# Lightning attention and a SMELU feed-forward block on one core: k and q of chunks 8 to 23 are cast into one tile and transposed by a crossbar DMA on SyncE's queue, and all v block copies go to Pool's queue

## The chip, the cores and the metric

One Trainium2 chip, one core. The metric is the device time of one execution in microseconds (us). Single executions of one kernel on one chip differ by 1 to 2%, so every kernel here was timed in rounds beside the kernel before on the same chip.

The engines: TensorE (PE in the profile; PEld is its weight load), VectorE (DVE), ScalarE (ACT), GpSimd (POOL) and SyncE (SP, which only issues DMAs here). All of them take their instructions in program order, each from its own list. "SPq" in the profile is SyncE's own list; "L259" is a line of the kernel file, and the numbers shift by some lines from kernel to kernel.

## The reference, cut to what matters

```python
# q, k, v: (4, 8, 768, 64) f32; lam: one decay per head
for b in range(nb):                       # blocks of 64 positions
    qb, kb, vb = ...
    intra = (qb @ kb^T * Dmask) @ vb      # Dmask: lam ** (i - j), causal
    inter = (qb * lam_pow) @ kv_state
    out = intra + inter
    kv_state = lam ** 64 * kv_state + (kb * rev_pow)^T @ vb
x = out as (3072, 512)
h = x @ w_in                              # 512 -> 2048
g = where(h >= 1, h, where(h <= -1, 0, (h + 1)**2 / 4))
return g @ w_out                          # 2048 -> 512
```

## The kernel before

The kernel cuts the attention into 24 chunks of 128 positions (6 for each of 4 batches). A chunk c goes through these steps: loads of k, q and v (256 KB each), casts of k and q to bf16 on ACT, eight PE transposes of 128x128 into PSUM (`t`), copies of the transposed k into a block layout (`kb`) and a product of the transposed q with a decay table (`qT`) on DVE, score matmuls (`s`), masks (`m`), output matmuls (`o`). From chunk 4 on the scaled v is also copied into a block layout by four small DMAs (`vb`, 32 KB each). Between these stand the two large products of the feed-forward block, `l1` (to `ph`) and `l2` (to `py`), which fill PE for most of the time.

```python
def cast(c, x, e):
    d, nm = ((qs, "qs"), (ks, "ks"))[x]
    t = qkp.tile([128, H, D], BF16, name=nm, tag=nm)
    ...                                   # ACT copy (chunk 0: DVE)
def f_vb(c, g, hi):
    o, i = vi[c % NV][HD[hi], :, g, hi, :], vn[c % NV][HD[g], :, hi, :]
    (nc.gpsimd if c < VP else nc.sync).dma_start(out=o, in_=i)          # VP = 12
def f_t(c):
    ptt[c] = pp_t.tile([128, 2, HP, 128], BF16, name="pt", tag="pt")    # PSUM
    for i, x in ((1, ks), (0, qs)):
        for hp in range(HP):
            nc.tensor.transpose(out=ptt[c][:, i, hp, :], in_=pair(x[c], hp), identity=ident)
def f_kb(c, hi):
    ...
    nc.vector.tensor_copy(kbd[c % NKB][HD[hi], :, :, hi, :], ptt[c][HD[hi], 1]...)
def f_qT(c):
    nc.vector.tensor_tensor(qT[c], ptt[c][:, 0], tab_q[:, c % NCB], op=AX.mult)
```

What stands in which engine's list, and where, is decided by a plan that runs when the kernel is built. Each operation is added with its engine, a duration in ns, a further `extra` until its result is there, the operations that it needs, and a due time; the plan then plays the engines forward, takes on each the ready operation that is due first, and writes the lists in that order. On the chip the lists are fixed: an instruction that is not ready holds up all that stand behind it (e9 below shows it on SyncE's list).

```python
add(key, "SP" if sp else "POOL", 600 if sp else 900 ..., fn, need, due=0, extra=1250 ...)   # issue of a load
add(("vb", c, i), "SP", 600, lambda ...: f_vb(...), need, due=-0.5, extra=2200)             # c >= VP
add(("t", c), "PE", mm(*[128] * 8), lambda c=c: f_t(c), [casts, kb and qT of c - 1], due=od - 9000, extra=FILL)
```

Of the kernel before, what the change touches and what calls it, by code (L numbers as in the profile page):

```python
# [9 lines left out]
BF16 = mybir.dt.bfloat16  # L10
I32 = mybir.dt.int32
AX = mybir.AluOpType
# [11 lines left out]
def kernel(  # L24
# [16 lines left out]
    nc = tc.nc  # L41
    B, H, S, D = q.shape
    C = 128
    NCB = S // C
    HP = H // 2
# [8 lines left out]
    CPS = MS // C  # L54

    PLAIN, KA = 4, 1
# [4 lines left out]
    const = ctx.enter_context(tc.tile_pool(name="const", bufs=1))  # L61
    big = ctx.enter_context(tc.tile_pool(name="big", bufs=1))
    ld = ctx.enter_context(tc.tile_pool(name="ld", bufs=LD))
    qkp = ctx.enter_context(tc.tile_pool(name="qkp", bufs=3))
    qtp = ctx.enter_context(tc.tile_pool(name="qtp", bufs=3))
    scp = ctx.enter_context(tc.tile_pool(name="scp", bufs=4))
    xp = ctx.enter_context(tc.tile_pool(name="xp", bufs=3))
# [2 lines left out]
    op = ctx.enter_context(tc.tile_pool(name="op", bufs=3))  # L70
# [30 lines left out]
    NKB, NUB, NV = 3, 3, 4  # L101
    kbd = [const.tile([128, HP, 2, 2, D], BF16, name=f"kbd{i}") for i in range(NKB)]
# [28 lines left out]
    for hi in range(2):  # L131
        nc.scalar.activation(out=ln_t[64 * hi:64 * hi + 64], func=AF.Ln,
                             in_=lam_b[64 * hi:64 * hi + 64].rearrange("p (a b) -> p a b", b=2)[:, :, hi])
# [5 lines left out]
    tab_q = const.tile([128, NCB, HP, 128], F32)  # L139
# [20 lines left out]


    spin = pp_y.tile([128, MS], F32, name="py", tag="py")
    LAT, FILL, SLACK, DSLACK, AHEAD = 70, 170, 400, 2500, 5000
    ops, OPS = [], {}

    class Op:
# [3 lines left out]
    def add(key, eng, ns, fn, needs=(), due=None, extra=0):  # L170
        OPS[key] = Op(key, eng, ns, fn, needs, due, extra)
        ops.append(OPS[key])

    def run_plan(free):

        users = {x.key: [] for x in ops}
        for x in ops:
            x.needs = [OPS[y] for y in x.keys if y in OPS]
            for y in x.needs:
                users[y.key].append(x)  # L180
        left = {x.key: len(x.needs) for x in ops}
        topo = [x for x in ops if not x.needs]
        for x in topo:
            for u in users[x.key]:
                left[u.key] -= 1
                if left[u.key] == 0:
                    topo.append(u)
        assert len(topo) == len(ops)
        for x in reversed(topo):
            d = [u.due - u.ns - x.extra - LAT for u in users[x.key] if u.eng not in ("DMA", "SP")]  # L190
            x.due = min(d + ([x.own] if x.own is not None else []), default=1e9)
            if x.eng in ("DMA", "SP") or x.key[0] in ("l1", "l2", "li", "wi", "zv"):
                x.due = x.own
        left = {x.key: len(x.needs) for x in ops}
        ready = {e: [] for e in free}
        for x in topo:
            if not x.needs:
                ready[x.eng].append((0, x))
        out_seq, pool_end = [], 0
        while len(out_seq) < len(ops):  # L200
            t, e = min((max(free[e], min(r for r, _ in lst)), e) for e, lst in ready.items() if lst)
            r, x = min(((r, x) for r, x in ready[e] if r <= t), key=lambda p: (p[1].due, p[0]))
            ready[e].remove((r, x))
            ns = x.ns
            if e == "DVE" and t < pool_end:
                if x.key[0] == "g1":
                    ns += pool_end - t
                elif x.key[0] in ("g2", "g"):
                    ns += min(ns, (pool_end - t) / 2)
            if e == "POOL":  # L210
                pool_end = t + ns
            free[e] = t + ns
            x.t, x.end = t, t + ns + x.extra
            out_seq.append((t, len(out_seq), x))
            for u in users[x.key]:
                left[u.key] -= 1
                if left[u.key] == 0:
                    lat = SLACK if u.eng == "PE" and x.end > 30000 else DSLACK if u.eng == "SP" else LAT
                    rel = u.own - AHEAD if u.key[0] == "t" and u.key[1] >= CPS else 0
                    ready[u.eng].append((max([rel] + [y.t if y.eng == u.eng else y.end + lat for y in u.needs]), u))  # L220
        pe_end = 1500
        for t, _, x in sorted(out_seq, key=lambda p: p[:2]):
            if x.eng == "PE":
                if x.key[0] == "l2":
                    pe_end = 1e9
                for _ in range(int((t - pe_end - 60) // (216 if t > 8000 else 430))):
                    nc.tensor.matmul(spin, lhsT=idle[:, 0:128], rhs=idle, start=True, stop=True)
                pe_end = max(pe_end, t + x.ns)
            if DBG:
                print(f"{t / 1e3:9.3f} {x.due / 1e3:9.3f} {x.eng:5s} {x.ns:6.0f} {x.key}")  # L230
            x.fn()

    def mm(*cols):
        return sum(c / 2.4 + 3 for c in cols)


    qs, ks, qT, sc_sb, xT, ptt, pst, pot = {}, {}, {}, {}, {}, {}, {}, {}
    pu = [None]
    HD = [slice(0, 64), slice(64, 128)]

# [1 line left out]
        return t[:, 2 * hp:2 * hp + 2, :].rearrange("p a d -> p (a d)")  # L242

    def cast(c, x, e):
        d, nm = ((qs, "qs"), (ks, "ks"))[x]
        t = qkp.tile([128, H, D], BF16, name=nm, tag=nm)
        if e == "ACT":
            nc.scalar.copy(out=t, in_=qkv_ld[c, x])  # L248
        else:
            nc.vector.tensor_tensor(t, qkv_ld[c, x], qkv_ld[c, x], op=AX.max)  # L250
        d[c] = t

    def cast_v(c):
        nc.gpsimd.tensor_tensor(vn[c % NV].rearrange("p a b d -> p (a b) d"), qkv_ld[c, 2],  # L254
                                _bc(tab_k[:, c % NCB, :], 2, D), op=AX.mult)

    VP = 12

    def f_vb(c, g, hi):  # L259
        o, i = vi[c % NV][HD[hi], :, g, hi, :], vn[c % NV][HD[g], :, hi, :]  # L260
# [1 line left out]

    def f_t(c):
        ptt[c] = pp_t.tile([128, 2, HP, 128], BF16, name="pt", tag="pt")
        for i, x in ((1, ks), (0, qs)):
            for hp in range(HP):
                nc.tensor.transpose(out=ptt[c][:, i, hp, :], in_=pair(x[c], hp), identity=ident)  # L267

    def f_kb(c, hi):
        if c < PLAIN:  # L270
            (nc.scalar.copy if c < KA else nc.vector.tensor_copy)(out=kplain(c), in_=ptt[c][:, 1])  # L271
        else:
            nc.vector.tensor_copy(kbd[c % NKB][HD[hi], :, :, hi, :], ptt[c][HD[hi], 1].rearrange("p a (b d) -> p a b d", b=2))  # L273

    def kplain(c):
        return kbd[c % NKB][:, 0:2].rearrange("p a b c d -> p (a b c d)").rearrange("p (h k) -> p h k", k=128)

    def f_qT(c):
        qT[c] = qtp.tile([128, HP, 128], BF16, name="qT", tag="qT")
        nc.vector.tensor_tensor(qT[c], ptt[c][:, 0], tab_q[:, c % NCB], op=AX.mult)  # L280

    def f_u(c):
        if c % NCB == 0:
# [103 lines left out]
        nc.sync.dma_start(out=out[m0:m0 + 128, :], in_=osb[s, ms])  # L387


    T0, STEP, LEAD = 24000, 1047, 3000  # L390
    PARTS = (4, 4, 4, 2, 2, 2)
    l1_order, l2_order = [], []
    for s in range(NST):
        if s == 0:
            o = [(0, 0), (1, 0), (0, 4), (1, 4), (2, 0), (2, 4), (0, 8), (1, 8), (2, 8), (2, 12), (0, 12), (1, 12), (3, 0), (3, 4), (3, 8), (3, 12)]
        else:
            o = [(p, i) for p in range(PARTS[s]) for i in range(0, FO, PARTS[s])]
        l1_order += [(s, i, p) for p, i in o]
        o = [(ms, kg) for ms in range(CPS) for kg in range(CPS)]
        if s == 0:  # L400
            o = [(ms, kg) for kg in range(CPS) for ms in range(2)] + o[FO // 2:]
# [9 lines left out]
    def o_due(c):  # L411
        s, i = c // CPS, c % CPS
        w = CPS // PARTS[s]
        return l_due[1, s, 0, i // w] - LEAD - (w - 1 - i % w) * 8 * STEP
# [14 lines left out]
    for kind, i in order:  # L429
        for x in (1, 0, 2) if kind == "c" else (0,):  # L430
            sp = kind == "c" and not (0 < i < SW or (i, x) == (0, 2))
            if kind == "w":
                key, land, ns, fn, need = ("wi", i), ("w", i), 2800, lambda i=i: load_w(i), []
            else:
                key, land, ns, fn = ("li", i, x), ("ld", i, x), 1060 if sp else 720 if i < 2 else 800, lambda i=i, x=x: f_load(i, x)
                need = [("cast", i - LD, x), ("w", 7) if i == SW else None]
# [18 lines left out]
    for c in range(NCH):  # L455
        od, cb = o_due(c), c % NCB
        lastu = c - 1 if cb else c - 2
        for x in (1, 0):
            e = "DVE" if c == 0 else "ACT"
            add(("cast", c, x), e, 690 if e == "DVE" else 615, lambda c=c, x=x, e=e: cast(c, x, e),  # L460
                [("ld", c, x), ("t", c - 3), ("u", c - 3), ("cast", c - 1, x)])
        for hp in range(HP) if c < NCB and c % 2 == 0 else ():
            add(("tab", c, hp), "ACT", 410, lambda c=c, hp=hp: tabq(c, hp), [("tab", c, hp - 1), (None, ("kb", 0, 0), ("x", 1))[c // 2]])
        add(("cast", c, 2), "POOL", 1060, lambda c=c: cast_v(c),
# [1 line left out]
        for i in range(4 if c >= PLAIN else 0):  # L466
            need = [("cast", c, 2), ("o", c - NV), ("zv", c % NV)]
            if c < VP:
                add(("vb", c, i), "POOL", 640, lambda c=c, i=i: f_vb(c, i // 2, i % 2), need, extra=2800)
            else:  # L470
                add(("vb", c, i), "SP", 600, lambda c=c, i=i: f_vb(c, i // 2, i % 2), need, due=-0.5, extra=2200)
        add(("t", c), "PE", mm(*[128] * 8), lambda c=c: f_t(c),
            [("cast", c, 0), ("cast", c, 1), ("kb", c - 1, 0), ("kb", c - 1, 1), ("qT", c - 1)], due=od - 9000, extra=FILL)
        for hi in range(1 if c < PLAIN else 2):
            add(("kb", c, hi), "ACT" if c < KA else "DVE", 590 if c < KA else 430 if c < PLAIN else 415, lambda c=c, hi=hi: f_kb(c, hi), [("t", c), ("s", c - NKB, 1), ("z", "kb", c % NKB) if c >= PLAIN else None])
        add(("qT", c), "DVE", 690, lambda c=c: f_qT(c), [("t", c), ("o", c - 3), ("qT", c - 1)] + [("tab", c // 2 * 2, hp) for hp in range(HP) if c < NCB])
        if cb < NCB - 1:
            add(("u", c), "PE", mm(*[128] * 4), lambda c=c: f_u(c),
                [("cast", c, 1), ("cast", c, 2), ("ub", lastu, 0), ("ub", lastu, 1), ("u", lastu)], due=od - 6000, extra=FILL)
# [66 lines left out]
```

## Time and profile before

| | kernel before |
|---|---|
| time, median of 3 (range) | 229.05 us (228.72 to 229.09) |
| profiled span | 227.0 us |
| PE busy | 217.0 us, 96% |
| eight PE transposes on the chain of waits | 0.45 us |
| v block copies issued by Pool / SyncE | 32 / 48 |

The page of the kernel before: the busy times, and rows of the span in 40 slices of 5.7 us (a digit is the busy share in tenths; PEclk is the granted TensorE clock in tenths; DMA is the mean busy share of the 16 DMA engines).

```profile
span 227.0 us, 5657 instructions
PE 217.0 (96%) x2272; PEld 158.7 (70%) x2308; DVE 159.5 (70%) x276; ACT 136.6 (60%) x249; POOL 74.0 (33%) x95
...
PE   7799999989999999999999999999999999999993
...
PEclk9999999999999999999999999999999999999999
DMA  5999998969999999497687732112101101110212
...
q1 hardware_dynamic: 71632, 21.77, 38.8%
q0 software_dynamic: 6768, 10.23, 20.5%
...
PE 78%; DVE 12%; POOL 4%; DMA 3%; issue 1%; ACT 0%; POOLq 0%; ACTq 0%
```

PE is busy 80% or more in every slice from 11 us on but the last, at full clock, and the chain of waits (its last line here) is PE for 78%. The DMA engines are full, too, for most of the first 16 slices (91 us): loads, weights and copies. PE waited only 0.2 us for them.

The windows view of the kernel before, 20 us each. Columns: stretch, its length, then busy us and number of instructions of PE, PEld, DVE, ACT and POOL, granted clock, DMA share, GB/s.

```profile
60.00:80.00 20.00, 19.47 (x276) 16.13 (x279) 19.08 (x28) 16.05 (x33) 15.37 (x20) 1.00 1.09 256
80.00:100.00 20.00, 19.49 (x266) 15.69 (x268) 18.82 (x35) 14.23 (x26) 4.04 (x3) 1.00 0.87 204
```

Three pieces of the chain in order of time (start, length, what; 54 to 62 us):

```profile
54.95 1.79 PE ph L339 x32
...
57.94 0.89 PE ph L339 x16
58.83 0.45 PE pt L267 x8
```

The group table gives 219 ns to a transposing matmul, which is its pipelined latency; on the chain eight of them take 0.45 us, and that is what PE gets back if they go.

### The profile page before, as it was taken

The numbers are of one execution on the slowest core, as the hardware profiler recorded it, in microseconds if no ns is written. First come the engines' busy times: TensorE is split into PE (matmuls) and PEld (weight loads), VectorE is DVE, ScalarE is ACT, GpSimd is POOL, SyncE is SP. The second block draws the span as 40 slices with busy tenths as digits, with TensorE's granted clock in tenths as the row PEclk, the third lists the DMA queues.
The fourth block names the chain that finished last, engine by engine and source line by source line (L and its number), as shares of the span: only waits on it lengthen the run. The fifth ranks groups of instructions, "written<-read, shape, count | busy, mean of one in ns | idle before, by whom it ended". The sixth has DMA issues, their size and how long they took to land.

```text
span 227.0 us, 5657 instructions
## 1 busy us (share of the span) xinstructions
PE 217.0 (96%) x2272; PEld 158.7 (70%) x2308; DVE 159.5 (70%) x276; ACT 136.6 (60%) x249; POOL 74.0 (33%) x95
## 2 busy tenths in 40 slices
PE   7799999989999999999999999999999999999993
PEld 2467888867787778877877777776777776766441
DVE  6635889998689998996678687783875775544300
ACT  6768575844988667588547648645565554545121
POOL 8999765956899420221032210000000000000000
PEclk9999999999999999999999999999999999999999
DMA  5999998969999999497687732112101101110212
GB/s 147 232 255 212 268 204 220 201 144 275 269 253 272 243 271 238 76 241 155 163 194 149 198 88 70 37 35 69 48 3 46 49 0 49 48 46 3 92 46 92
DMA packets 78570, 32.36 MB, mean 143 GB/s; under 512 B 69648, under 2 KB 73744, under 8 KB 78544
## 3 DMA queue, kind: packets, MB, share of 16 engines
q1 hardware_dynamic: 71632, 21.77, 38.8%
q0 software_dynamic: 6768, 10.23, 20.5%
q8 instruction: 18, 0.29, 0.5%
q14 instruction: 8, 0.07, 0.1%
q10 hardware_dynamic: 144, 0.00, 0.0%
HBM read 27.27 MB, written 6.29 MB: 148 GB/s over the span
## 4 chain that ended last, share of the span: by engine, by line
PE 78%; DVE 12%; POOL 4%; DMA 3%; issue 1%; ACT 0%; POOLq 0%; ACTq 0%
PE ph L339 32%; PE py L378 32%; PE pt L267 4%; DVE gT L372 3%; DMA w_in_sb<-in_moe_w_in_dram 3%; PE ps L298 3%; DVE t L353 3%; PE po L322 2%; DVE w L357 2%; PE po L316 2%; PE pu L286 2%; DVE sc L309 1%; POOL x2f L420 1%; DVE kbd L273 1%; POOL vn L254 1%
## 5 line engine op out<-in xcount | busy, mean ns | idle before, releaser
L347 ACT ACTIVATE r<-ph,one 128x512 bf16<-128x512 f32 x96 | 65.8, 687 | 60.5 <-PE ph L339 42.2
L339 PE MATMUL ph<-xT,w_in_sb 128*128 128x128 bf16 (+1 forms) x1152 | 98.9, 237 | 0.2 <-DMA w_in_sb<-in_moe_w_in_dram 0.2
L339 PEld LDWEIGHTS <-w_in_sb 128*128 128x128 bf16 x1152 | 81.7, 98 | 15.5 <-DMA w_in_sb<-in_moe_w_in_dram 0.4
L378 PE MATMUL py<-w_out_sb,gT 128*128 128x512 bf16 x351 | 89.8, 379 | 1.7
L378 PEld LDWEIGHTS <-gT 128*128 128x128 bf16 x384 | 34.6, 98 | 27.5
L254 POOL TENSOR_TENSOR vn<-x2f,tab_k 128x512 bf16<-128x512 f32 x24 | 27.6, 1151 | 52.2 <-DMA vi<-vn 22.7
L353 DVE TENSOR_SCALAR t<-r 128x1024 bf16<-128x1024 bf16 x48 | 25.3, 526 | 23.8 <-ACT r L347 23.7
L372 DVE TENSOR_TENSOR gT<-w,t 128x1024 bf16<-128x1024 bf16 x48 | 37.3, 778 | 1.1
L357 DVE TENSOR_TENSOR w<-r,t 128x1024 bf16<-128x1024 bf16 x48 | 35.4, 738 | 1.4
L309 DVE TENSOR_TENSOR sc<-ps,causal 128x512 bf16<-128x512 f32 (+1 forms) x40 | 22.1, 553 | 7.4 <-PE ps L298 7.4
L383 ACT COPY osb<-py 128x512 f32<-128x512 f32 x24 | 14.0, 585 | 15.7 <-PE py L378 15.2
L273 DVE COPY kbd<-pt 64x512 bf16<-64x512 bf16 x40 | 16.8, 419 | 7.1 <-PE pt L267 6.7
L261 POOL DMA_DIRECT2D vi<-vn x32 | 20.2, 647 | 2.7 <-POOL vn L254 2.4
L280 DVE TENSOR_TENSOR qT<-pt,tab_q 128x512 bf16<-128x512 bf16 x24 | 16.6, 690 | 1.7 <-ACT kbd L271 1.1
L329 ACT CAST xT<-po 128x512 bf16<-128x512 f32 x24 | 14.0, 583 | 5.6 <-PE po L322 4.1
L290 ACT CAST ubd<-pu 64x256 bf16<-64x256 f32 x40 | 14.6, 365 | 2.4 <-PE pu L286 2.1
L248 ACT CAST qs<-x0f 128x512 bf16<-128x512 f32 x23 | 14.2, 618 | 0.7 <-DMA x0f<-in_q_dram 0.7
L298 PE MATMUL ps<-qT,kbd 128*128 128x128 bf16 (+1 forms) x160 | 13.3, 206 | 1.4 <-DVE qT L280 0.8
L248 ACT CAST ks<-x1f 128x512 bf16<-128x512 f32 x23 | 14.2, 616 | 0.1
L316 PE MATMUL po<-qT,ubd 128*128 128x128 bf16 x80 | 13.8, 221 | 0.0
L298 PEld LDWEIGHTS <-kbd 128*128 128x128 bf16 x160 | 10.5, 98 | 4.4 <-issue 1.5
L322 PE MATMUL po<-sc,vi 128*128 128x128 bf16 (+1 forms) x160 | 13.2, 206 | 0.1
(50 smaller groups left out, 136.2 us busy)
## 6 DMA issues: line engine op xcount, KB each, us to landing
out_dram<-osb SPq DMA_DIRECT2D x24, 256.0 KB, 2.0
x1f<-in_k_dram SPq DMA_DIRECT2D x18, 256.0 KB, 4.1
x0f<-in_q_dram SPq DMA_DIRECT2D x18, 256.0 KB, 4.3
x2f<-in_v_dram SPq DMA_DIRECT2D x17, 256.0 KB, 4.1
w_in_sb<-in_moe_w_in_dram POOLq DMA_DIRECT2D x4, 512.0 KB, 7.5
w_out_sb<-in_moe_w_out_dram POOLq DMA_DIRECT2D x4, 512.0 KB, 9.8
x2f<-in_v_dram POOLq DMA_DIRECT2D x7, 256.0 KB, 4.7
x1f<-in_k_dram POOLq DMA_DIRECT2D x6, 256.0 KB, 6.6
```

What stands on the lines that cost most here:

```text
L248: nc.scalar.copy(out=t, in_=qkv_ld[c, x])
L254: nc.gpsimd.tensor_tensor(vn[c % NV].rearrange("p a b d -> p (a b) d"), qkv_ld[c, 2], _bc(tab_k[:, c % NCB, :], 2, D), op=AX.mult)
L261: (nc.gpsimd if c < VP else nc.sync).dma_start(out=o, in_=i)
L273: nc.vector.tensor_copy(kbd[c % NKB][HD[hi], :, :, hi, :], ptt[c][HD[hi], 1].rearrange("p a (b d) -> p a b d", b=2))
L298: nc.tensor.matmul(pst[c, g][:, hp, :], lhsT=kbd[c % NKB][:, hp, g].rearrange("p a d -> p (a d)"), rhs=qT[c][:, hp, 64 * g:], start=True, ...
L309: nc.vector.tensor_tensor(sc_sb[c][g], pst[c, g], _bc(causal[:, 0:128 - 64 * g], 1, HP), op=AX.mult)
L339: nc.tensor.matmul(ph[:, j * m:(j + 1) * m], lhsT=w_in_sb[:, ko, (i + j) * 128:(i + j + 1) * 128], rhs=xT[s][:, ko, p * m:(p + 1) * m], st ...
L347: nc.scalar.activation(out=r_t[grp][:, i, :], in_=ph_t[s, ni, part], func=AF.Relu, bias=one[:, 0:1])
L353: nc.vector.tensor_scalar(t_t[grp], r_t[grp], 0.5, 1.0, op0=AX.mult, op1=AX.min)
L357: nc.vector.tensor_tensor(w_t[grp], r_t[grp], t_t[grp], op=AX.subtract)
L372: nc.vector.tensor_tensor(o, w, t, op=AX.mult)
L378: nc.tensor.matmul(py_t[s, ms], lhsT=gT[s][:, ko, ms * 128:(ms + 1) * 128], rhs=w_out_sb[:, ko, :], start=(ko == 0), stop=(ko == FO - 1))
```

## The change

Intent: PE is full, DMA has been carrying less from 100 us on, so the transposes of chunks 8 to 23 move from PE to the DMA crossbar. k and q share one tile so that one DMA of 256 KB does both. The result lies in SBUF in place of PSUM, which should make DVE's copies cheaper. The v block copies leave SyncE's queue to make room for the transposes.

```diff
-    qkp = ctx.enter_context(tc.tile_pool(name="qkp", bufs=3))
+    NQK, NXT, XT = 4, 2, 8
+    qkp = ctx.enter_context(tc.tile_pool(name="qkp", bufs=NQK))
+    xtp = ctx.enter_context(tc.tile_pool(name="xtp", bufs=NXT))
...
+    def f_xt(c):
+        t = xtp.tile([128, 2, HP, 128], BF16, name="xq", tag="xq")
+        ptt[c] = t
+        nc.sync.dma_start_transpose(out=t..., in_=qk[c].rearrange("p a h d -> p (a h d)"))
...
-    VP = 12
+    VP = 24
...
-    T0, STEP, LEAD = 24000, 1047, 3000
+    T0, STEP, LEAD = 24000, 1015, 3000
...
+        if c < XT:
+            add(t, "PE", mm(*[128] * 8), lambda c=c: f_t(c), need, due=od - 9000, extra=FILL)
+        else:
+            add(t, "SP", 1250, lambda c=c: f_xt(c), need, due=-0.7, extra=3500)
```

Cut: the shared tile `qk` in the casts and their due times, the release of a transpose 16 us (of plan time) before the chunk's output is due at the earliest, the DVE durations told to the plan.

## The prediction

> **What bounds the kernel now.** TensorE (PE). The page's first part has PE busy 217.0 us of the 227.0 us span at a granted clock of 0.999. The chain of waits is PE for 78%, and after 85 us almost nothing else. VectorE (DVE) is the second limit: 12% of the chain, in two stretches, about 38 to 48 and 68 to 85 us. The windows view has DVE busy 42.8 of 47 us between 38 and 85 us, but 57.3 of 75 between 85 and 160; Pool 33.1, then 9.5.
>
> **What the change takes away.** 128 transposing matmuls and their weight loads (16 chunks of 8); the built program's order shows exactly these 256 PE instructions gone. The group table gives 219 ns for one, but that is pipelined latency: on the chain eight take 0.45 us. So 16 x 0.45 = 7.2 us of PE time. About 14 of the 16 lie after 80 us, where PE bounds: 6.3 us. The plan's pace constant falls by 32 ns over 192 steps, 6.1 us, which agrees.
>
> DVE's k copies (32 half-tiles at 419 ns from PSUM) now read SBUF. A one-source SBUF copy of twice the row length takes 408 to 426 ns here, so I estimate 0.26 us: 5 us less DVE work. The q product stays at 690 ns.
>
> **What it adds.** 16 crossbar transposes of 256 KB on SyncE's queue. The Trainium skill (VectorE: DVE Perf Modes, "The three transpose paths") gives 1309 ns for a 128x128 block by DMA; no transpose is in this trace, so the cost of eight blocks is open. The nearest things are stores landing in 2.0 us and loads in 4.1 to 4.3. I estimate 3 to 6 us from issue to landing, hidden: the plan releases it 14 us before the chunk's output is due, about 8 us before its scores.
>
> 48 block copies of v move to Pool at 0.64 us each: 31 us more Pool work, mostly between 75 and 165 us, where Pool has room. DVE pays: the skill (SBUF — State Buffer, "Who interferes with whom") says that Pool and DVE's fast modes lock each other out of a shared port. The trace agrees: DVE's three gate steps take 0.43, 0.69 and 0.69 us while Pool is quiet, up to 2.05, 1.41 and 2.26 while it works. Their excess is about 11 us for some 42 us of Pool work after 20 us, so 31 us more should cost about 8 us, less the 5 saved. DVE goes from 76% to perhaps 80 to 85% after 85 us: below PE, with a few longer stalls.
>
> **On the critical path.** 7.2 us off; I give back 0.5 to 1 us for copies drawn into the DVE-bound stretch and for jitter. Predicted: 222.7 us (-2.8%), range 219.8 to 227.0. Faster by over 2% (below 224.5): 0.68; within 2%: 0.25; slower by over 2%: 0.07.
>
> **What would show it.** PE busy about 210 us, the chain after 85 us still PE; transposing matmuls down from 192 to 64; Pool busy about 105 us; k copies from chunk 8 near 0.26 us; more long gate steps after 85 us; transposes landing within 6 us, and score matmuls waiting little for qT. Wrong if score matmuls wait for transposes, PE shows over 2 us more idle, or SyncE's stores and loads stand behind transposes.
>
> **What would make it wrong.** Transposes that take 8 us or more, or hold up the loads on DMA engines that are full (share about 1.0) until 85 us; Pool falling behind, since a chunk's copies and scaling need about 3.7 us of it and DVE can block it; DVE stalls on Pool reaching PE between 68 and 100 us. Better than predicted if cheaper k copies shorten the DVE-bound stretch.

## More of the kernel before

32 matmuls of `l1` take 1.79 us, 16 take 0.89.

And two lines of SyncE's timeline, with 17 loads between them (start, length of the issue, what):

```profile
59.17 1.03 SPq L420 DMA_DIRECT2D x0f<-in_q_dram  x1
...
79.75 0.78 SPq L420 DMA_DIRECT2D x0f<-in_q_dram  x1
```

From 59.17 to 79.75 us SyncE issues nothing but prefetch loads, one every 1.14 us (20.58 us over 18). The plan reckons with 0.6. In this kernel PE waits for none of these loads.

## The result, and the profile after

The changed kernel took 237.54 us (median of 4, 236.64 to 238.51) beside 229.07 us for the kernel before: 1.037 times the time (95% interval 1.033 to 1.042). All four runs count as fast, at a mean granted clock of 0.971 to 0.983. Ratios here and below are the mean time of one kernel's fast runs over that of the other's of the same rounds, so not quite the ratio of the medians that are quoted.

```profile
span 236.7 us, 5411 instructions
PE 217.4 (92%) x2180; PEld 154.8 (65%) x2180; DVE 159.5 (67%) x276; ACT 137.3 (58%) x249; POOL 104.4 (44%) x143
...
PE   7897999999994794898999999999999999999993
...
PEclk9999999999999799799999999999999999999999
DMA  5999997969999999999999514372433011100212
...
q1 hardware_dynamic: 75472, 24.39, 46.4%
...
PE 56%; DMA 18%; DVE 17%; POOL 3%; ACT 2%; issue 1%; SPq 0%; ACTq 0%; POOLq 0%
PE py L386 24%; PE ph L347 23%; DMA xq<-qk 11%; DVE w L365 4%; DVE t L361 4%; DMA w_in_sb<-in_moe_w_in_dram 4%; DVE gT L380 3%; DVE sc L317 2%; PE ps L306 2%; DVE kbd L281 2%; DMA x2f<-in_v_dram 2%; PE po L330 2%; DVE qT L288 2%; PE po L324 1%; DMA vi<-vn 1%
```

The chain is now PE for 56% only, and 11% of it is the new transposes (`DMA xq<-qk`). PE has two holes between 71 and 95 us (the digits 4, 7, 9, 4), the clock dips as each ends, and the DMA engines stay full six slices longer, to 130 us. The same stretches as before:

```profile
60.00:80.00 20.00, 14.68 (x190) 11.56 (x188) 12.60 (x20) 13.97 (x27) 14.30 (x20) 0.97 1.11 248
80.00:100.00 20.00, 15.72 (x170) 12.14 (x169) 9.93 (x19) 8.61 (x16) 7.14 (x10) 0.86 1.22 251
```

PE lost 4.8 us of work between 60 and 80 us and 3.8 us between 80 and 100 us against before, and from 80 to 100 us the mean clock was 0.86. What PE waited for, by the view of waits (line, releaser: us in total, times, longest), and what DVE waited for:

```profile
PE ps L306 <- DVE qT L288: 10.1, 4, 5.3
```

```profile
DVE kbd L281 <- DMA xq<-qk: 17.0, 5, 6.7
```

The kernel before had 0.8 us of the first and of course none of the second. Now the two long waits in PE's timeline (start, length, what, and in brackets the idle time before it and its releaser):

```profile
78.68 0.58 PE L306 MATMUL ps<-qT,kbd 128*128 128x128 bf16 x4 [5.26 <-DVE qT L288]
79.06 1.91 PE L386 MATMUL py<-w_out_sb,gT 128*128 128x512 bf16 x4
80.77 1.69 PE L347 MATMUL ph<-xT,w_in_sb 128*128 128x128 bf16 x16
82.30 0.28 PE L306 MATMUL ps<-qT,kbd 128*128 128x64 bf16 x4
...
95.70 0.60 PE L306 MATMUL ps<-qT,kbd 128*128 128x128 bf16 x4 [4.16 <-DVE qT L288]
96.10 3.41 PE L347 MATMUL ph<-xT,w_in_sb 128*128 128x128 bf16 x32
```

Waits of 5.26 and 4.16 us, both for `qT` of a chunk whose transpose had just landed. And after each of them PE runs at half speed for a while: 16 matmuls of `l1` start at 80.77 and are followed by the next group at 82.30, 1.53 us, where 16 of them took 0.89 us in the kernel before; 32 take 3.25 us from the start at 96.10 to that of the next group, in place of 1.79. Over the stretches 78.7 to 82.3 and 95.7 to 99.4 us that costs some 3 us (the sum of these differences and that of the four `py` matmuls, 1.71 for 0.86). The Trainium skill (TensorE: Matmul & The Clock Gate, "What's actually happening") says that TensorE falls to half clock after an idle window of about 3.4 us and comes back after a busy one of about 3.4 us; this trace agrees, with idle times of 5.3 and 4.2 us and half speed for 3.6 us after each (the windows view has a clock of 0.50 from 97 to 99 us and 1.00 from 99.4 us on). In the other traces of this case the bound is less sharp: all 13 waits of PE over 4 us were followed by half clock, but so was one of 2.59 us (e6), while one of 3.69 us (e9) was not.

So why did the transposes come late? The last cast of chunk 8 on ACT, then SyncE's own timeline:

```profile
61.57 0.62 ACT L252 CAST qk<-x0f 128x512 bf16<-128x512 f32 x1
```

```profile
66.17 2.29 SPq L428 DMA_DIRECT2D x1f<-in_k_dram  x1
...
70.56 1.29 SPq L428 DMA_DIRECT2D x1f<-in_k_dram  x1
71.93 1.99 SPq L259 DMA_TRANSPOSE xq<-qk  x1
...
77.84 1.99 SPq L259 DMA_TRANSPOSE xq<-qk  x1
```

And all transposes (counts, ns, first and last start; the first line is SyncE's own waiting before them):

```profile
L259 SPq EVENT_SEMAPHORE  x16: 17/17/28, 71.9 to 180.9; - x16
L259 SPq DMA_TRANSPOSE xq<-qk x16: 1293/1359/3207, 71.9 to 181.0; - x16
...
DMA to landing us min/median/max: 2.7/4.4/6.7
```

The casts of chunk 8's k and q were done by 62.2 us. Its transpose was issued at 71.93 us, because SyncE was issuing prefetch loads back to back, about 1 us each, and the transpose stood behind them in the list; once it was at the head it did not wait (17 to 28 ns). The plan's own listing puts that transpose at 61.0 us of plan time, behind loads reckoned at 600 ns of issue each. The shortest issue of a load takes 0.37 us in these traces, and a store's takes 0.34 us in the quiet after 140 us; between 50 and 126 us, with the DMA engines full, a load's takes a median of 0.85 us plus about 0.1 us until the next. Over twenty loads SyncE falls some 10 us behind its plan. The landing itself takes 2.7 to 6.7 us, median 4.4. A late transpose holds up ACT as well as DVE: a cast writes one of four shared `qk` tiles and must wait until the transpose that reads it has landed (10.9 us of ACT's waiting here).

What the prediction foresaw did happen beside this: Pool is busy 104.4 us, the k copies from SBUF have a median of 291 ns, and DVE's three gate steps cost 102.5 us in place of 98.0.

### The profile page after: what moved, and what is told of

It is laid out like the page before. It is cut to its first block, busy times and chain, and to the rows that moved or that the text cites. A ratio compares the mean times of both kernels' runs of the same rounds, so it can differ in the third digit from the quotient of the medians.

```text
span 236.7 us, 5411 instructions
## 1 busy us (share of the span) xinstructions
PE 217.4 (92%) x2180; PEld 154.8 (65%) x2180; DVE 159.5 (67%) x276; ACT 137.3 (58%) x249; POOL 104.4 (44%) x143
## 3 DMA queue, kind: packets, MB, share of 16 engines
q1 hardware_dynamic: 75472, 24.39, 46.4%
## 4 chain that ended last, share of the span: by engine, by line
PE 56%; DMA 18%; DVE 17%; POOL 3%; ACT 2%; issue 1%; SPq 0%; ACTq 0%; POOLq 0%
PE py L386 24%; PE ph L347 23%; DMA xq<-qk 11%; DVE w L365 4%; DVE t L361 4%; DMA w_in_sb<-in_moe_w_in_dram 4%; DVE gT L380 3%; DVE sc L317 2%; PE ps L306 2%; DVE kbd L281 2%; DMA x2f<-in_v_dram 2%; PE po L330 2%; DVE qT L288 2%; PE po L324 1%; DMA vi<-vn 1%
## 5 line engine op out<-in xcount | busy, mean ns | idle before, releaser
L347 PE MATMUL ph<-xT,w_in_sb 128*128 128x128 bf16 (+1 forms) x1152 | 101.3, 240 | 2.8 <-DMA w_in_sb<-in_moe_w_in_dram 1.9
L386 PE MATMUL py<-w_out_sb,gT 128*128 128x512 bf16 x384 | 96.3, 382 | 0.0
L347 PEld LDWEIGHTS <-w_in_sb 128*128 128x128 bf16 x1152 | 83.7, 100 | 18.0 <-DMA w_in_sb<-in_moe_w_in_dram 2.2
L269 POOL DMA_DIRECT2D vi<-vn x80 | 50.3, 645 | 54.6 <-issue 49.6
L361 DVE TENSOR_SCALAR t<-r 128x1024 bf16<-128x1024 bf16 x48 | 26.6, 554 | 23.6 <-ACT r L355 23.5
L365 DVE TENSOR_TENSOR w<-r,t 128x1024 bf16<-128x1024 bf16 x48 | 38.5, 802 | 1.3
L306 PE MATMUL ps<-qT,kbd 128*128 128x128 bf16 (+1 forms) x160 | 13.7, 210 | 10.7 <-DVE qT L288 10.1
L281 DVE COPY kbd<-xq 64x512 bf16<-64x512 bf16 x32 | 10.4, 325 | 17.4 <-DMA xq<-qk 17.0
L252 ACT CAST qk<-x1f 128x512 bf16<-128x512 f32 x23 | 14.2, 618 | 11.2 <-DMA xq<-qk 10.9
L252 ACT CAST qk<-x0f 128x512 bf16<-128x512 f32 x23 | 14.1, 619 | 0.2 <-DMA x0f<-in_q_dram 0.2
L229 PE MATMUL py<-idle 128*128 128x512 bf16 x36 | 11.6, 462 | 1.2 <-DVE one L117 1.2
```

The lines of the kernel that those rows point to most:

```text
L252: nc.scalar.copy(out=t, in_=qkv_ld[c, x])
L306: nc.tensor.matmul(pst[c, g][:, hp, :], lhsT=kbd[c % NKB][:, hp, g].rearrange("p a d -> p (a d)"), rhs=qT[c][:, hp, 64 * g:], start=True, ...
L347: nc.tensor.matmul(ph[:, j * m:(j + 1) * m], lhsT=w_in_sb[:, ko, (i + j) * 128:(i + j + 1) * 128], rhs=xT[s][:, ko, p * m:(p + 1) * m], st ...
L361: nc.vector.tensor_scalar(t_t[grp], r_t[grp], 0.5, 1.0, op0=AX.mult, op1=AX.min)
L365: nc.vector.tensor_tensor(w_t[grp], r_t[grp], t_t[grp], op=AX.subtract)
L386: nc.tensor.matmul(py_t[s, ms], lhsT=gT[s][:, ko, ms * 128:(ms + 1) * 128], rhs=w_out_sb[:, ko, :], start=(ko == 0), stop=(ko == FO - 1))
```

## The experiments

Theories, formed after reading the trace:

- **Q**: the transposes stand too late in SyncE's in-order list, behind loads that the full DMA engines accept at 1 us each and not at 0.6.
- **P**: the 31 us of extra Pool issues lock DVE out, and that starves PE.
- **L**: a landing time of 4.4 us hurts wherever the transpose stands.
- **D**: the DMA engines cannot carry loads and transposes together.
- **R** (formed later): what matters is the order of the compute engines, not SyncE's.

Eighteen kernels ran, all with correct results. Overview (median us of all runs, with the slow ones in e3, e4, e6, e9, e11, e15, e16 and e17; ratio of fast runs to the kernel before on the same chip, 95% interval; PE's total wait for `qT` in the profiled run):

| run | edit to the changed kernel | us | ratio | wait for qT |
|---|---|---|---|---|
| (changed) | none | 237.5 | 1.037 (1.033 to 1.042) | 10.1 |
| e1 | transposes back on PE, v copies on Pool | 229.9 | 1.008 (0.999 to 1.018) | none listed |
| e2 | v copies back on SyncE | 242.9 | 1.063 (1.056 to 1.071) | 12.0 |
| e3 | plan: load issue 1050 | 230.4 | 1.007 (0.997 to 1.016) | 5.9 |
| e4 | transposes from chunk 14 on | 235.4 | 1.028 (1.017 to 1.038) | 8.8 |
| e5 | transposes on ScalarE's queue | 249.9 | 1.091 (1.085 to 1.098) | 0.5 |
| e6 | e4 with load issue 1050 | 230.0 | 1.002 (0.993 to 1.011) | 2.7 |
| **e7** | plan: load 1150, transpose 2000 + 5000 | **222.3** | **0.970 (0.962 to 0.977)** | none listed |
| e8 | e7, transposes from chunk 12 on | 224.9 | 0.982 (0.977 to 0.988) | 0.6 |
| e9 | SyncE's order of e7, others as changed | 259.1 | 1.127 (1.116 to 1.138) | 0.7 |
| e10 | SyncE's order as changed, others of e7 | 235.8 | 1.028 (1.020 to 1.036) | 1.0 |
| e11 | plan: load 1150 only | 226.2 | 0.978 (0.968 to 0.989) | 0.3 |
| e12 | plan: transpose 2000 + 5000 only | 234.9 | 1.022 (1.015 to 1.030) | 8.4 |
| e13 | every transpose six places earlier | 240.7 | 1.049 (1.041 to 1.058) | 8.4 |
| e14 | e7 with v copies back on SyncE | 224.6 | 0.977 (0.969 to 0.985) | 1.0 |
| e15 | e5 with slower loads in the plan | 231.2 | 0.999 (0.988 to 1.010) | 1.4 |
| e16 | transposes of chunks 8 to 13 earlier | 239.0 | 1.042 (1.031 to 1.052) | 0.2 (see below) |
| e17 | transposes of chunks 8 to 16 earlier | 230.0 | 1.002 (0.995 to 1.010) | 1.5 |
| e18 | e7 again, five rounds | 222.8 | 0.972 (0.966 to 0.978) | 0.8 |

The profiled runs of e3, e4 and e15 fell in the slow state of those kernels' runs (over 1.5% above their fastest); their traces are read for which wait stands where, and the ratios use fast runs alone.

### e1_pool_only: the v copies alone

```diff
-    NQK, NXT, XT = 4, 2, 8
+    NQK, NXT, XT = 4, 2, 24
```

> All chunks are transposed by TensorE again (128 transposing matmuls back); only the 48 v block copies stay moved to Pool, with the one tile for k and q. Theory Q (the crossbar transposes stand behind prefetched loads in SyncE's in-order queue and reach PE late): no transposes, so 228 to 231 us and PE's wait for qT near zero, as before. Theory P (Pool's 31 us of extra issues lock DVE out, and that starves PE): 234 us or more, with DVE's gate steps long between 80 and 150 us.

229.9 us, ratio 1.008: within the noise of the kernel before, with 31 us more Pool work. P is out. This run also gives what a transpose costs the DMA engines, as it differs from the changed kernel's traffic by the 16 transposes alone:

```profile
span 226.6 us, 5611 instructions
...
q1 hardware_dynamic: 58576, 20.19, 34.5%
q0 software_dynamic: 8304, 11.80, 23.3%
```

SyncE's queue took 34.5% of 226.6 us here, 78.2 us of all sixteen engines, for 77 loads and stores of 256 KB: 1.02 us each. In the changed kernel it took 46.4% of 236.7 us, 109.8 us. The 16 transposes are the difference, 31.6 us: **1.98 us of packet time on all sixteen engines for each transpose of 256 KB**, about twice a load. (Packets that wait for each other are counted in full, as a share of 1.22 shows, so this is rather too much than too little; e5 gives a second value.)

### e2_xt_only: the transposes alone

```diff
-    VP = 24
+    VP = 12
```

> The 16 crossbar transposes stay, the 48 v block copies go back to SyncE's queue, where they take 0.6 us of issue each. Theory Q: the loss stays, 235 to 245 us, with PE waiting about 10 us for qT between 70 and 100 us; it may grow, as the copies share the transposes' queue. Theory P: the loss goes, 222 to 226 us.

242.9 us: the loss stays and grows, PE waits 12.0 us for `qT`. It is the transposes, and freeing SyncE's queue of the v copies helped them, as the change intended.

### e3_li1050: one number of the plan

```diff
-            add(key, "SP" if sp else "POOL", 600 if sp else ...
+            add(key, "SP" if sp else "POOL", (1050 if i else 600) if sp else ...
```

> The changed kernel with one number of its plan altered: an issue of a load on SyncE is reckoned at 1050 ns, about what the trace shows while DMA engines are full, in place of 600. No work is added or taken away; the transpose of chunk 8 has 17 SyncE instructions ahead of it, not 23. Theory Q: the first transpose is issued by 66 us (71.9 in the changed kernel), PE's waits for qT fall from 10.1 to under 3 us, and the time is 221 to 227 us. Theory P, or a theory L that a transpose's 4.4 us of landing is what hurts wherever it stands: within 1% of 237.5 us.

230.4 us, ratio 1.007. The first transpose was issued at 67.7 us and PE's waits fell to 5.9 us: 3% back by reordering alone, which speaks for Q against P and L, though less than Q expected (under 3 us, 221 to 227 us).

### e4_xt14: start later

```diff
-    NQK, NXT, XT = 4, 2, 8
+    NQK, NXT, XT = 4, 2, 14
```

> Crossbar transposes only from chunk 14 on (10 in place of 16), all v copies on Pool as in the changed kernel. Most of these are due after 105 us, when the DMA engines' share falls below 0.8 and few loads remain. Theory Q: PE's wait for qT under 1.5 us; 10 x 0.45 us = 4.5 us of PE time saved against before, so 224 to 226.5 us. Theory P: still 232 us or more. Theory L: each transpose still lands late, 228 us or more.

A miss for the way I had put Q: 235.4 us. The quiet of the DMA engines that I had counted on did not come in time (they were full until about 118 us in this trace), and SyncE's list had fallen behind by then. The first transpose, chunk 14's, was issued at 110.85 us after an unbroken run of loads and a few stores, and PE's one long wait was 7.32 us just before that chunk's scores; after it there was none over 1.2 us. Q has to be said more exactly: the lag of SyncE's list grows with every load, and whatever stands behind the loads gets all of it.

### e5_act_queue: another queue

```diff
-        nc.sync.dma_start_transpose(...)
+        nc.scalar.dma_start_transpose(...)
-            add(t, "SP", 1250, lambda c=c: f_xt(c), need, due=-0.7, extra=3500)
+            add(t, "ACT", 1250, lambda c=c: f_xt(c), need, extra=3500)
```

> The 16 crossbar transposes are issued by ScalarE on its own queue, in its order of work, in place of SyncE's queue; everything else is the changed kernel's. Theory Q (place in SyncE's in-order queue): a transpose no longer waits its turn behind loads, so chunk 8's is issued by about 65 us, PE waits for qT under 2 us in all, 221 to 227 us, though ScalarE gives some 1.3 us of issue for each. Theory D (the DMA engines are full, and each transpose takes about 2 us of all sixteen of them wherever it is issued): transposes still land 4 to 6 us late and PE still waits over 5 us for qT, 232 us or more.

Both theories missed. Chunk 8's transpose was issued at 64.2 us and the wait for `qT` went (0.5 us), as Q said; but the time was 249.9 us. Now ACT stood with casts at the head of its list, 20.7 us for transposes that had to free a `qk` tile and 7.8 us for the loads x0f and x1f, and what PE waited for stood behind them.

```profile
PE pu L294 <- ACT ubd L298: 12.3, 4, 6.7
```

The transposes landed after 5.0 us (median), no faster than on SyncE's queue. Alone on ACT's queue, their packets took 10.2% of 248.5 us, 1.58 us for each (1.83 us in e15), which is less than the difference in e1 gives. The Trainium skill (DMA: Bandwidth & Descriptors, "Issuing engines are not separate DMA queues") says that DMAs of all issuing engines run on the same 16 engines and interleave, so that several issuers only save issue time; this run agrees.

### e6_li1050_xt14 and e8_li1150_xt2000_from12: later starts with a corrected plan

e6 is e4 plus e3's edit; e8 is e7 (next) with `XT = 12`.

> e4_xt14 (transposes from chunk 14 on) with the plan's issue of a load on SyncE reckoned at 1050 ns in place of 600, as in e3. Theory Q: the one long wait of e4 (7.3 us before chunk 14's scores) falls under 2 us and the time to 224 to 228 us. Theory D: a wait of 5 us or more stays, 232 us or more.

> As e7, with transposes from chunk 12 on (12 of them). Theory Q and D both: less DMA work before 100 us, PE's wait for qT under 2 us, and 12 x 0.45 = 5.4 us of PE time off the kernel before: 223.5 to 226.5 us. If PE still waits over 4 us for qT, neither an accurate order nor a later start cures it.

e6: 230.0 us, the 7.3 us wait fell to 2.6 us; better than e4 by 2.5%, though short of 224 to 228. e8: 224.9 us, as expected; that it is slower than e7 fits twelve transposes saving less PE time than sixteen.

### e7_li1150_xt2000: the plan told what the DMA engines do

```diff
-            add(key, "SP" if sp else "POOL", 600 if sp else ...
+            add(key, "SP" if sp else "POOL", (1150 if i else 600) if sp else ...
-            add(t, "SP", 1250, lambda c=c: f_xt(c), need, due=-0.7, extra=3500)
+            add(t, "SP", 2000, lambda c=c: f_xt(c), need, due=-0.7, extra=5000)
```

> The changed kernel (16 transposes from chunk 8 on) with its plan told what the full DMA engines do: 1150 ns for an issue of a load on SyncE, 2000 ns for that of a transpose and 5000 ns more until it has landed (600, 1250 and 3500 in the changed kernel). Only the order of instructions changes. Theory Q: PE's wait for qT falls from e3's 5.9 us to under 3, 223 to 228 us. Theory D: no better than e3's 230 us, as loads then come late in place of transposes.

222.3 us, ratio 0.970: faster than both kernels, with the same instructions and the same bytes as the changed kernel, in another order.

```profile
span 218.2 us, 5364 instructions
PE 209.5 (96%) x2148; PEld 151.5 (69%) x2180; DVE 157.6 (72%) x276; ACT 137.1 (63%) x249; POOL 104.8 (48%) x143
...
PEclk9999999999999999999999999999999999999999
DMA  5999999668999999999999999925532110111112
```

```profile
63.03 3.47 SPq L259 DMA_TRANSPOSE xq<-qk  x1
...
67.22 2.11 SPq L259 DMA_TRANSPOSE xq<-qk  x1
```

The transpose of chunk 8 now goes out at 63.0 us (71.9), that of chunk 9 at 67.2 (77.8). No wait of PE for `qT` is left in the view of waits, the clock stays at full, PE is busy 209.5 us. Two theories fall here. L: the landing takes 4.7 us (median), longer than in the changed kernel, and hurts nobody. D: the DMA engines are full until about 142 us (the row of digits) and carry everything in time.

### e11_li1150 and e12_xt2000: which number

e11 has only the first of e7's two edits, e12 only the second.

> e7 with only one of its numbers: an issue of a load is reckoned at 1150 ns, a transpose at 1250 and 3500 again. If the loads' number is what matters: within 1.5% of e7, 220 to 226 us. If the transposes' own 2 us of DMA time had to be known to the plan too: 227 to 232 us, like e3 (230.4).

> e7 with only the other numbers: a transpose is reckoned at 2000 ns of issue and 5000 more to landing, a load at 600 again; SyncE has 23 instructions ahead of the first transpose, as in the changed kernel. Theory Q: the first transpose is still issued after 70 us, PE waits 7 us or more for qT, 231 us or more. If the landing time alone was the mis-sized number: 221 to 227 us.

e11: 226.2 us (0.978; two of its four runs are slow, the fast ones took 223.6 and 225.2 us). e12: 234.9 us (1.022), first transpose at 71.3 us, 8.4 us of waits. The number that was wrong for the plan is the issue of a load; the transposes' own numbers may add a little once that is right (0.970 for e7, but the intervals overlap). How far a few per cent hang on it is shown by e3 (1050 ns: 1.007) and e11 (1150 ns: 0.978). So the number is to be taken as a handle on the order, not as a duration to be measured to 10%.

### e9_sync_order_alone and e10_compute_order_alone: whose order

The plan is made twice, with both sets of numbers, and the lists are taken from one or the other:

```diff
+        sp, rest = plan(free, SP_TOLD), plan(free, REST_TOLD)
+        seq = {e: [(t, x) for t, x in (sp if e == "SP" else rest) if x.eng == e] for e in free}
```

SP_TOLD and REST_TOLD say which plan is told e7's numbers: True and False in e9, False and True in e10. With both from the first plan this gives the changed kernel's lists instruction for instruction, with both from the second e7's. In e9 SyncE's exact list of e7 would deadlock with the other engines' old lists, so where nothing can go on, the next SyncE instruction that can is taken (moves of one or two places).

> The plan is made twice, with the changed kernel's numbers and with e7's. TensorE, ScalarE, VectorE and Pool follow the changed kernel's order exactly; only SyncE's 84 instructions follow e7's order (where that would deadlock, the instruction is moved by one or two places). Theory Q (SyncE's order is the cause): e7's time is had from this alone, 221 to 227 us, with PE waiting under 3 us for qT. Rival R (e7 won because its compute engines put other work in the transposes' place): little is won, 233 us or more.

> The mirror of e9: TensorE, ScalarE, VectorE and Pool follow e7's order, SyncE that of the changed kernel, with 23 instructions before the first transpose. Theory Q: PE still waits 8 us or more for qT and the time is 232 to 245 us. Rival R: 221 to 227 us.

e10: 235.8 us, inside Q's range, but not in the way that Q said: PE waited 1.0 us for `qT`, not 8. The transposes do go out late, at 70.7, 79.0 and 89.8 us, about as in the changed kernel. But PE's one long wait, 6.84 us, is for ACT's `xT`, and ACT had stood before that for a store:

```profile
ACT osb L405 <- DMA out_dram<-osb: 12.8, 1, 12.8
```

The store was issued at 88.65 us, behind loads in SyncE's old list, and e7's compute order wants its buffer back earlier. So e10 shows that e7's compute order does not give e7's time with SyncE's old list, but not that the transposes are the reason.

e9 missed by far: 259.1 us.

```profile
64.97 1.42 SPq L447 DMA_DIRECT2D x1f<-in_k_dram  x1
71.25 0.36 SPq L414 DMA_DIRECT2D out_dram<-osb  x1
...
75.82 1.26 SPq L447 DMA_DIRECT2D x0f<-in_q_dram  x1
81.99 0.36 SPq L414 DMA_DIRECT2D out_dram<-osb  x1
```

SyncE stands still from 66.4 to 71.25 us and from 77.1 to 82 us. The instructions at which it stands are stores of a finished output: e7's list has them ahead of loads because e7's PE finishes those outputs earlier. With the old compute order they were not finished, and the loads behind them came late (ACT waited 38 us for x0f and x1f). The wait for `qT` was nearly gone (0.7 us), as Q said, but e9 is not the clean test of Q that I had meant: in both runs a store stands in the wrong place for the other lists.

### e13, e16 and e17: only the transposes moved

The clean test keeps every other list as it is, and loads and stores in their order among themselves; only transposes move forward in SyncE's list, one place at a time while no deadlock follows.

```diff
+        for c in range(XT, LAST):          # e13: all;  e16: up to 13;  e17: up to 16
+            i = next(i for i, x in enumerate(sp_q) if x.key == ("xt", c))
+            for _ in range(N):             # e13: 6;  e16, e17: 6, 8, then 11 (chunk 16 in e17: 4)
+                new = sp_q[:i - 1] + [sp_q[i], sp_q[i - 1]] + sp_q[i + 1:]
+                if sp_q[i - 1].key[0] not in ("li", "st") or not stands(new):
+                    break
+                sp_q, i = new, i - 1
```

> The changed kernel, all engines in its own order, with one edit to SyncE's: each transpose stands up to six instructions earlier (17 ahead of chunk 8's in place of 23); loads and stores keep their order among themselves. Theory Q: the transpose of chunk 8 is issued by about 66 us (71.9), the 5.3 us wait of PE before chunk 8's scores falls under 1.5 us, and the time falls to 225 to 233 us (237.5). If place is not the cause, or if what is gained is lost on later loads as in e9: 236 us or more.

> The changed kernel, all other engines in its own order; on SyncE only the transposes of chunks 8 to 13 stand earlier, by 6, 8 and then up to 11 instructions; those from chunk 14 on, the loads and the stores keep their order. Theory Q: PE's waits for qT fall from 10.1 us to under 4, no half-clock stretch, 226 to 233 us (237.5). If place alone is not worth much: 235 us or more.

> As e16, with the transposes of chunks 14, 15 and 16 earlier too (by up to 11, 11 and 4 instructions), so that none of those among loads keeps its place; every other engine and the order of loads and stores among themselves are the changed kernel's. Theory Q: no wait of PE over 3 us after the first 60 us, 225 to 232 us (237.5). If the wait only moves on to another transpose or to a late load again: 235 us or more, and place alone is not enough without an order of the other engines that fits it.

e13, 240.7 us, missed. Its first wait was gone: the transpose of chunk 8 went out at 64.9 us, and PE's first long wait, 4.46 us, came at 90.1 us, for chunk 10's. But from 121 us on transposes now stood before stores and the last loads, where they waited for a free buffer:

```profile
SPq L296 <- DVE qT L325: 43.2, 7, 8.7
```

The stores came late, ACT waited 18.3 us for them, and PE lost what it had won: busy 63.4 us between 60 and 130 us (59.1 in the changed kernel), but 53.9 between 130 and 190 us (59.4).

e16, 239.0 us, missed too, in an instructive way. At 110 us it had started 735 matmuls of `l1` (a 256-column one counted as two) and 120 of `l2`, the changed kernel 665 and 104, the kernel before 742 and 108 (its trace lacks 33 records of `l2`): it was ahead of the changed kernel. Then came chunk 14, the first whose transpose had been left in its place, issued at 114.05 us behind thirteen loads and stores in a row. In PE's and DVE's timelines:

```profile
120.55 0.59 PE L343 MATMUL ps<-qT,kbd 128*128 128x128 bf16 x4 [7.36 <-DVE sc L354]
```

```profile
118.85 0.59 DVE L318 COPY kbd<-xq 64x512 bf16<-64x512 bf16 x2 [8.68 <-DMA xq<-qk]
```

The wait simply moved to the first transpose that still stood behind the loads, and took all. (PE's line names a mask, `sc`, as the releaser; DVE's line shows that DVE itself stood 8.68 us for the transpose.)

e17 moves those of chunks 14 to 16 as well:

```profile
PE ps L343 <- DVE qT L325: 1.5, 2, 1.2
```

230.0 us, no wait of PE over 1.4 us after 60 us, and full clock. That is 7.5 us off the changed kernel's 237.5 by moving nine DMA instructions forward and nothing else, inside Q's range (in ratios to the kernel before, 1.037 and 1.002; the two did not run beside each other).

### e14 and e15: what else is needed

e14 is e7 with `VP = 12`. e15 is e5 with 1400 ns for a load's issue and for its transfer, and 5000 to a transpose's landing.

> e7 with the 48 v block copies back on SyncE's queue (each reckoned at 600 ns there, though they cost more while the DMA engines are full). If moving them to Pool is a needed part: SyncE has 29 us more of issue in the same stretch, transposes come late again, 228 us or more. If not: within 1.5% of e7's 222.3 us, and Pool's 31 us of issue could be saved.

> e5 (transposes on ScalarE's queue) with its plan told that a load takes 1400 ns of issue and 1400 ns of transfer (600 and 1060 in e5) and that a transpose lands 5000 ns after its issue (3500). If e5's 250 us came of ScalarE standing in its order before casts of loads that were late: 222 to 232 us, with ScalarE waiting under 8 us for loads. If the DMA engines cannot carry both streams: 240 us or more.

e14: ratio 0.977, against 0.970 and 0.972 for e7 (e18 below), with overlapping intervals: with a plan that fits, no gain from the move of the v copies to Pool is clear of the noise, and it is not what makes the change pay. e15: 231.2 us in place of 249.9, with ACT waiting 4.2 us for loads and 4.3 for transposes: ScalarE's queue, too, lost by order in the main and not by the DMA engines, and it is still no better than the kernel before.

### e18_e7_again

> e7 unchanged, with five rounds: 220 to 224.5 us, 2 to 4% below the kernel before.

222.8 us, ratio 0.972 (0.966 to 0.978), in other rounds, beside e17: e7 holds.

## Why the prediction was wrong

It said 222.7 us and 2.8% faster; the changed kernel took 237.5 us and was 3.7% slower.

**What was right.** PE does lose its transposes: e7, the same instructions without the stalls, has PE busy 209.5 us in one trace and 210.5 in the other (217.0 before; predicted about 210; each of these traces lacks some 32 to 36 matmul records, so it is the difference that counts, 6.5 to 7.5 us for 7.2 predicted) and takes 222.3 and 222.8 us. The k copies fell to a median of 0.29 us (estimated 0.26). Pool was busy 104.4 us (105). DVE's gate steps rose by 4.5 us (98.0 to 102.5; estimated 8), and by 1.3 to 5.5 us in e1, e7 and e18. The landing time of a transpose, 4.4 us in the median, lay in the 3 to 6 us that were estimated, though it spread to 6.7.

**The step that failed** is this one: "I estimate 3 to 6 us from issue to landing, hidden: the plan releases it 14 us before the chunk's output is due, about 8 us before its scores." The landing was right and "hidden" was wrong, because a release in the plan was taken for an issue on the chip. Between them stands SyncE's list. The plan issues a load in 600 ns; with the DMA engines full, SyncE needed about 1 us, as the trace of the kernel before already showed (1.14 us from load to load between 59 and 80 us). In the kernel before the lag was harmless: loads run six chunks ahead, and what else stood on SyncE had slack. A transpose on the same list has 8 us of slack and meets a lag of 10. The prediction named the reverse as a risk (loads standing behind transposes); of its own signs of being wrong, it was the first that came, score matmuls waiting for transposes.

**Where the 15 us between e7 and the changed kernel lie.** The profiled spans are 236.7 us and, in e18, 221.7 us. PE's waits for `qT` are 10.1 us against 0.8, so 9.3; about 3 us are half-clock work after the two long waits; some 2.7 us are left, spread over small waits and pipeline gaps. That the plan's two numbers, and so the order of the lists, cause all of it is shown by e7, which changes nothing else. That the places of nine transposes on SyncE alone account for half (7.5 us) is shown by e17. The other half, from 230.0 to 222.3 us, comes when all lists are made together with the corrected numbers; e10 and e9, which were to say whose lists give it, were both spoiled by stores. How that half divides stays open.

**What the rivals came to.** P: e1. L: e7. D: e7 carries the same bytes in time; but SyncE issues slowly where the DMA engines are full, so they probably belong to the cause (seen together in the traces, not tested alone). R, as the whole cause: e17, which leaves the compute engines' lists as they were; its share of the other half is open.

## What to carry to other kernels

When work moves from a compute engine to a DMA, ask where the new DMA will stand in the issuing engine's in-order list, and measure in the trace of the old kernel how fast that list really drains while the DMA engines are full; prefetch loads that nobody waits for can hold up a transfer that everybody waits for. If a planner or a hand-made order places the instructions, correct its durations from a trace of the loaded machine before judging the change: here one constant (600 to 1150 ns) was worth 5%, and turned a loss into a gain. And in every trace here a stall of PE of over 4 us was paid for again, at half clock, after it had ended.

## What the Trainium skill lacked or had wrong

- Advanced Engine Details and Errata, "X-Bar Transpose (TRN2)": it says that transpose DMAs are as fast as regular ones (350 to 400 GB/s). Here a transpose of 256 KB from SBUF to SBUF took 1.98 us of packet time on all sixteen engines, about 132 GB/s, and a load or store of 256 KB 1.02 us (changed kernel against e1; e4, with ten of them, gives 1.97 by the same sum); on a queue of their own it was 1.58 and 1.83 us (e5, e15), up to 166 GB/s. Part of that may be time in which packets wait for each other on full engines. DMA: Bandwidth & Descriptors ("Latency and other measured facts") has 261 GB/s for a transpose with a non-contiguous middle dimension, which is also above it.
- DMA: Bandwidth & Descriptors, "Issuing engines are not separate DMA queues": it calls the issuer's time "usually small relative to the DMA itself". I found nothing on that page on how it grows with load: SyncE's issue of a 256 KB load took 0.37 us at the shortest and 0.85 us in the median with the engines full, up to 2.3 us, and one of a transpose 1.3 to 3.2 us. The plan reckoned without this growth.
- VectorE: DVE Perf Modes, "The three transpose paths": 1309 ns for a 128x128 block by DMA. Eight blocks in one DMA landed in 2.7 us (median after 130 us, where the engines' mean share is 0.35), so the figure is not one to be multiplied.
- No page that I read has it: the same 32 KB v block copy is 272 packets from SyncE's queue and 32 from Pool's (q1 falls by 13056 packets for 48 copies from the kernel before to e1, q0 rises by 1536), and costs 0.21 and 0.13 us of all engines.
